# Written tables for the order of five engines in a fused recurrent attention and two-layer kernel

## The chip, the cores and the metric

The kernel runs on one core of one Trainium2 chip. The metric is the device time of one execution in microseconds (us). A core has five engines that run their own lists of instructions in order and wait for each other by semaphores: PE (TensorE, matmuls), ACT (ScalarE), DVE (VectorE), POOL (GpSimd) and SP (SyncE, which here only issues DMA transfers). POOL issues some transfers too.

## The reference

A gated linear recurrence over 768 tokens, for 4 batches of 8 heads with 48 channels each, and a two-layer network on its output.

```python
for t in range(S):
    state = alpha[:, :, t, :, None] * state + np.einsum('bhd,bhe->bhde', k[:, :, t], v[:, :, t])
    y[:, :, t] = np.einsum('bhd,bhde->bhe', q[:, :, t], state)
x = np.ascontiguousarray(y.transpose(0, 2, 1, 3)).reshape(B * S, H * D)
h = x @ w_in                      # 3072 x 384 by 384 x 2048
r = np.maximum(h, 0.0)
out = (r * r) @ w_out             # 2048 x 384
```

Inputs and output are float32; the kernel multiplies in bfloat16.

## The kernel before, in words

The work is cut into 12 units, g = 0 to 11: unit g is batch g mod 4 and the tokens 256 (g div 4) onward, so that units 4 to 7 go on with the states of units 0 to 3, and 8 to 11 with theirs. A unit takes these steps, and each step of the program has a short name with the unit's number, which the prediction uses:

- Loads: lda, ldk, ldq, ldv bring 384 KB each of alpha, k, q and v (L568). SP issues them, for unit 2 POOL. Two halves of w_in (win0, win1) and of w_out (wout0, wout1), 768 KB each, come by POOL's queue (L539). A load has a gate (`AFTER`, `BEHIND`): from unit 4 on all four loads of g wait until ldq of g-1 has landed; lda3 waits for wout0, win0 for lda1; from unit 5 on lda waits also for ln of the unit before, ldk for ekm, ldq and ldv until tr0 of the unit before has landed. SP waits for a gate at the place where the load stands in its list.
- Decays: pr multiplies pairs of alphas (DVE L675 or POOL L677), ln and lm take logarithms (ACT L678, L717), m1i and m1s sum them by a triangular matmul (PE L684, bank psW), ei, ea, ec and es are exponentials of these sums (ACT L695 to L721; units 0 and 1 have forms of their own, L584 to L667), bk, aq and lb are products and differences (DVE).
- ekm and eqm scale k and q (DVE L751, L746, L620). tr transposes them: units 0 to 2 on PE (L632, L774) with evictions et, from unit 3 on by two DMA transposes from SP, tr0 and tr1 (L762).
- p: scores, 32 small matmuls into psX and psZ (PE L940); mk0 and mk1 mask them on DVE (L951, 1.2 us each).
- vc: v to bfloat16 (ACT L742 or POOL L741, L613). y: output matmuls into psX, which from y2 to y10 also hold the state matmuls kv of unit g+1 and therefore need vc of g+1 (PE L832, L843, L811). sa, sc, sd update the states (sd on POOL L915 or DVE L917).
- xe evicts y (ACT L971), xt transposes it (PE L986 for units 0 to 3, a DMA transpose L992 from unit 4 on), xv copies (DVE L998).
- The dense part: s1 is eight blocks of six matmuls (PE L1042) into two banks psH in turn, each emptied by re (ACT L1050 or DVE L1052) and squared by sq (DVE L1060, ACT L1064); s2 is eight blocks of four matmuls (L1089) into psO, emptied by oe (ACT L1097, DVE L1099); out stores (SP L1109).

What sets the order: `add` records each step with its engine or engines to choose from, a cost, a priority, and what it depends on: writers of what it reads, readers of what it overwrites, and, of a PSUM bank (`ps`), all earlier readers of that bank too, so that two readers never meet there. `schedule` simulates the program with these costs and always takes the ready step of least priority; priorities carry hand offsets (`SHIFT`). `fill` then puts 37 matmuls on zeros (fillers, L1143) into PE's list where its simulation sees a gap before the first s1; they wait for the memset of the zero tile. `place` turns dependencies into semaphore waits, leaving out those that another wait already covers; a step of PE never waits for a step of PE, a step of ACT or DVE can wait for one of its own engine. `emit` writes the lists.

```python
            if k[0] == "ps":
                for r in self.readers.get(k, ()):
                    op.deps.setdefault(r, False)
...
                if d.sem is None and d.eng == o.eng == "pe":
                    continue
```

Of the kernel before, what the change touches and what calls it, by code (L numbers as in the profile page):

```python
# [2 lines left out]

# [28 lines left out]


class Program:

    HOP = 35
    PE_LATENCY = 170
    DMA_FIRST = {"sp": 1300, "act": 1300, "pool": 2000}  # L40
    PACKET = (("win", 172), ("wout", 490), ("ld", 22), ("tr", 18), ("xt", 18), ("out", 125))
    SBUF_ONLY = ("pr", "bk", "aq", "ekm", "eqm", "sq", "sb", "sd")
    BIAS = {"pool": 300}
    DMA_LAST = {"sp": 800, "act": 800, "pool": 1900}
    SWITCH = 95
# [1129 lines left out]
```

## Time and profile before

| what | value |
|---|---|
| runs | 176.59, 176.57, 174.76 us; median 176.57 |
| span of the profiled execution, first to last instruction | 174.5 us (the lowest run is 0.3 above it) |
| PE busy | 169.1 us, 97% |
| DVE, ACT, POOL busy | 121.3, 117.6, 18.8 us |
| s1 matmuls L1042 | 576, mean 275 ns |
| s2 matmuls L1089 | 368, mean 326 ns |
| fillers L1143 | 37, 10.5 us |
| DMA moved | 33.36 MB, mean 191 GB/s |
| HBM read, written | 25.17 MB, 4.72 MB |

The profile page gives busy time by engine, the span in 40 slices with a digit for the busy share in tenths, the chain of work that ended last, and groups of instructions with their number and mean time. A matmul's mean holds its way through the array, so that several overlap; what a block of matmuls costs is read from the start of one block to the start of the next. The trace names instructions by line; since every engine runs its list in order, the n-th instruction in the trace is the n-th of the list, and so each step of the program has its time.

### The profile page before, as it was taken

To read this page: it belongs to the slowest core of one execution; us is meant where nothing else is said; L and a number is where in the kernel's file an instruction comes from. 1 tells how busy PE (TensorE), PEld (TensorE's weight loads), DVE (VectorE), ACT (ScalarE), POOL (GpSimd) and SP (SyncE) were. 2 spreads that over 40 slices of the span, in tenths; PEclk is the share of its full clock that TensorE was granted. 3 is DMA by queue.
4 is the path that set the end of the run, shared out by engine and by line. 5 is a ranking of instruction groups with operands and counts; after the bars stand their busy time and mean duration, and the time that the engine had idled before them with its cause. 6 is when DMAs were issued, how large, how long until landed. Compare 5 with 4: busy or idle time off the path is not lost.

```text
span 174.5 us, 5094 instructions
## 1 busy us (share of the span) xinstructions
PE 169.1 (97%) x2237; PEld 130.5 (75%) x2237; DVE 121.3 (70%) x197; ACT 117.6 (67%) x211; POOL 18.8 (11%) x28
## 2 busy tenths in 40 slices
PE   7989999999999999999999999999999999999994
PEld 2556898856886697777788886778788697688773
DVE  5497799797967869866778966868849726322230
ACT  3848698868869569768768757378668564566440
POOL 3159010022102120000100000000200000000000
DMA  5999999979998999798998897999899690040022
GB/s 139 324 297 190 274 303 216 230 208 280 274 229 125 274 235 188 200 222 151 278 212 211 228 196 180 275 201 251 201 214 208 115 196 4 0 135 4 10 80 90
DMA packets 74743, 33.36 MB, mean 191 GB/s; under 512 B 71649, under 2 KB 71905, under 8 KB 74721
## 3 DMA queue, kind: packets, MB, share of 16 engines
q1 hardware_dynamic: 73184, 28.32, 71.4%
q0 software_dynamic: 1536, 4.72, 12.1%
q8 instruction: 17, 0.28, 0.7%
q14 instruction: 6, 0.04, 0.1%
HBM read 25.17 MB, written 4.72 MB: 171 GB/s over the span
## 4 chain that ended last, share of the span: by engine, by line
PE 56%; DMA 26%; ACT 6%; DVE 4%; SPq 3%; POOL 2%; issue 1%
PE psO L1089 22%; PE psWH L1042 22%; DMA raw<-in_v_dram 9%; DMA wout<-in_moe_w_out_dram 8%; DMA raw<-in_alpha_dram 5%; DMA raw<-in_q_dram 5%; SPq L568 3%; PE psO L1143 2%; POOL raw L568 2%; ACT rr L1050 2%; PE psX L843 2%; PE psX L1012 2%; ACT vbf L742 1%; PE psZ L811 1%; PE psX L832 1%; PE psX L940 1%
## 5 line engine op out<-in xcount | busy, mean ns | idle before, releaser
L1042 PE MATMUL psWH<-xt,win 128*128 128x256 bf16 x576 | 73.9, 275 | 0.5 <-ACT rr L1050 0.2
L1042 PEld LDWEIGHTS psWH<-xt,win 128*128 128x128 bf16 x576 | 65.0, 145 | 6.2 <-DVE rr L1052 1.6
L1089 PE MATMUL psO<-wout,gt 128*128 128x384 bf16 x368 | 68.9, 326 | 0.0
L1050 ACT ACTIVATE rr<-psWH 128x512 bf16<-128x512 f32 x83 | 48.9, 596 | 21.5 <-PE psWH L1042 20.0
L1089 PEld LDWEIGHTS psO<-wout,gt 128*128 128x128 bf16 x368 | 34.8, 98 | 18.3 <-DVE gt L1060 0.2
L1060 DVE TENSOR_TENSOR gt<-rr 128x1024 bf16<-128x1024 bf16 (+1 forms) x47 | 28.4, 608 | 25.1 <-ACT rr L1050 24.5
L951 DVE TENSOR_TENSOR pm<-psX,caus 128x1024 bf16<-128x1024 f32 x12 | 14.6, 1220 | 2.4 <-PE psZ L940 2.1
L951 DVE TENSOR_TENSOR pm<-psZ,caus 128x1024 bf16<-128x1024 f32 x12 | 14.6, 1216 | 1.5 <-PE psZ L940 1.4
L1097 ACT ACTIVATE osb<-psO 128x384 f32<-128x384 f32 x19 | 9.3, 489 | 6.8 <-PE psO L1089 6.3
L971 ACT ACTIVATE xbf<-psX 128x768 bf16<-128x768 f32 x12 | 9.7, 806 | 5.0 <-PE psX L832 4.1
L746 DVE TENSOR_TENSOR qks<-raw,eq 128x384 bf16<-128x384 f32 x18 | 10.3, 605 | 3.0 <-DMA raw<-in_q_dram 3.0
L1143 PE MATMUL psO<-zero 128*128 128x512 bf16 (+1 forms) x37 | 10.5, 417 | 1.3 <-DVE zero L489 1.3
L741 POOL CAST vbf<-raw 128x768 bf16<-128x768 f32 x4 | 3.7, 930 | 71.5 <-DMA raw<-in_v_dram 71.5
L1064 ACT ACTIVATE gt<-rr 128x512 bf16<-128x512 bf16 (+1 forms) x13 | 10.8, 828 | 0.4
L751 DVE TENSOR_TENSOR qks<-raw,ek 128x768 bf16<-128x768 f32 x11 | 10.7, 969 | 0.4 <-ACT ek L663 0.3
L1052 DVE TENSOR_SCALAR rr<-psWH 128x512 bf16<-128x512 f32 x13 | 8.9, 687 | 2.0 <-PE psWH L1042 1.6
L742 ACT ACTIVATE vbf<-raw 128x768 bf16<-128x768 f32 x7 | 5.9, 845 | 3.5 <-DMA raw<-in_v_dram 3.5
L717 ACT ACTIVATE la<-raw 128x384 f32<-128x384 f32 x8 | 4.2, 523 | 5.3 <-DMA raw<-in_alpha_dram 5.2
L1143 PEld LDWEIGHTS psO<-zero 128*128 128x128 bf16 x37 | 3.5, 108 | 4.6 <-issue 1.9
L906 DVE TENSOR_TENSOR smd<-psZ,sbd 128x384 bf16<-128x384 f32 x8 | 4.4, 554 | 3.4 <-PE psX L832 3.4
L675 DVE TENSOR_TENSOR prd<-raw 128x384 f32<-128x384 f32 x7 | 4.0, 569 | 2.9 <-DMA raw<-in_alpha_dram 2.9
L678 ACT ACTIVATE lab<-prd 128x384 bf16<-128x384 f32 x10 | 5.2, 520 | 1.1 <-POOL prd L677 0.6
(115 smaller groups left out, 165.9 us busy)
## 6 DMA issues: line engine op xcount, KB each, us to landing
raw<-in_alpha_dram SPq DMA_DIRECT2D x11, 384.0 KB, 4.2
raw<-in_k_dram SPq DMA_DIRECT2D x11, 384.0 KB, 5.1
raw<-in_q_dram SPq DMA_DIRECT2D x11, 384.0 KB, 4.2
raw<-in_v_dram SPq DMA_DIRECT2D x11, 384.0 KB, 4.8
out_dram<-osb SPq DMA_DIRECT2D x11, 384.0 KB, 4.3
win<-in_moe_w_in_dram POOLq DMA_DIRECT2D x2, 768.0 KB, 9.9
wout<-in_moe_w_out_dram POOLq DMA_DIRECT2D x2, 768.0 KB, 15.2
raw<-in_alpha_dram POOLq DMA_DIRECT2D x1, 384.0 KB, 9.7
```

Source lines behind the costliest of these rows:

```text
L746: add("dve", lambda e, j=j, dst=dst: e.tensor_tensor(dst, RAW[r][:, 2, :, j, :].rearrange("p (n x) d -> p n x d", x=2), EQ[la][:, j].rearr ...
L751: add("dve", lambda e, a=a, E=E: e.tensor_tensor(QKS[qs][:, a, :, :, 0:D], RAW[r][:, 1 + a].rearrange("p h j d -> p j h d"), E[la][:].rear ...
L951: add("dve", lambda e, hf=hf, psT=psT: e.tensor_tensor(PM[pm][:, hf].rearrange("p r n j t -> p (r n) (j t)"), psT[:, :, :].rearrange("p r ...
L971: add("act", lambda e: e.activation(XBF[x2][:], psX[:, :, 0:HD], AF.Copy), act_ns(2 * HD), p0 + 6100, reads=[("ps", "X", 0), ("ps", "X", 1 ...
L1042: ins = pe.matmul(psH[hb][:, i * T:(i + 1) * T], WIN[:, kk, hidden(fj)], mov, start=(kk == 0), stop=(kk == KT - 1))
L1050: add("act", lambda e, hb=hb, rr=rr: e.activation(rr, psH[hb], AF.Relu), act_ns(512), pu + 600, reads=[("ps", "H", hb)], writes=[("rr", rb ...
L1052: alts={"dve": (lambda e, hb=hb, rr=rr: e.tensor_scalar(rr, psH[hb], 0.0, None, ALU.max), dve_ns(512))})
L1060: add("dve", lambda e, dst=dst, sq=sq: e.tensor_tensor(dst, sq, sq, ALU.mult), 148 + k * 267, pu + 1200, reads=[("rr", rb, h) for h in ran ...
L1064: "act": (lambda e, dst=dst, sq=sq: e.activation(dst, sq, AF.Square), act_ns(k * 512))})
L1089: ins = pe.matmul(psS, GT[gt][:, fj, j, :], WOUT[:, fj, :], start=(fj * parts % FT == 0), stop=((fj + 1) * parts % FT == 0))
L1097: add("act", lambda e, j=j, psS=psS: e.activation(OSB[ob][:, j], psS, AF.Copy), act_ns(DM), ps_ + 700, reads=[keyS], writes=[("osb", ob, j ...
L1143: pr.fill(lambda n: lambda pe: pe.matmul(psO[:, 0:n], ZERO[:, 0:128], ZERO[:, 0:n], skip_group_check=True), ((512, 216, 420), (256, 109, 2 ...
```

## The change

The scheduler, its constants and its offsets go, and `fill` with them. The five orders stand in the kernel as text, `TABLES`, and `arrange` takes each step's engine and place from there; `+512` and `+256` in PE's table are fillers. `sequence` gives `place` an order of all steps that keeps every dependency. `place` leaves out one more kind of wait: of a step on an earlier step of its own engine when the only reason was that both read the same bank. Readers on different engines still wait for each other. The steps themselves, their tiles and their arithmetic are the same; 20 steps go from ACT to DVE and vc6 to POOL; 24 come to ACT from DVE, vc0 and vc5 from POOL; sd1, sd2, pr5 and pr6 go from POOL to DVE; POOL's list shrinks from 24 to 19, PE's fillers from 37 to 23.

```diff
                 for r in self.readers.get(k, ()):
-                    op.deps.setdefault(r, False)
+                    if r not in op.deps:
+                        op.deps[r] = False
+                        op.shared.add(r)
...
             for r in self.readers.get(k, ()):
                 if r is not op:
                     op.deps.setdefault(r, False)
+                    op.shared.discard(r)
...
-                if d.sem is None and d.eng == o.eng == "pe":
+                if d.sem is None and d.eng == o.eng and (o.eng == "pe" or not raw and d in o.shared):
                     continue
...
+    def arrange(self, tables, make, after):
...
+            for x in text.split():
+                if x[0] == "+":
+                    o = Op({e: (make(int(x[1:])), 0)}, 0, "fill")
...
+                    o.deps = {after: True}
...
+                o.eng = e
+                o.fn, o.cost = o.alts[e]
+                o.pos = len(self.order[e])
+                self.order[e].append(o)
```

The lists of before, for the places that the prediction names:

```
pool ... vc0 win0 win1 sd0 lda2 ldk2 ldq2 ldv2 wout0 wout1 sd1 pr3 sd2 vc4 pr5 vc5 pr6 vc7 vc10
sp   lda0 ldk0 ldq0 ldv0 lda1 ldk1 ldq1 ldv1 lda3 ldk3 ldq3 ldv3 lda4 ldk4 ldq4 ldv4 out0_1 tr0_3 tr1_3 lda5
     ldk5 tr0_4 tr1_4 ldq5 ldv5 out1_1 lda6 ldk6 tr0_5 tr1_5 out2_1 xt4 ldq6 ldv6 lda7 ldk7 tr0_6 tr1_6 xt5
     ldq7 ldv7 out3_1 lda8 ldk8 tr0_7 tr1_7 out4_1 xt6 ldq8 ldv8 ...
pe   9 fillers, m10_0 m11_0, 4 fillers, tr00_0, 2 fillers, tr10_0, 3 fillers, tr01_0 p0_0 kv0 tr11_0 ...
     y5 s2_3_1_0 s1_4_5 s2_3_1_1 s2_3_1_2 s1_4_7 s2_3_1_3 s1_4_4 m1i7 ...
act  table, xcaus, ln0_0 ln1_0 ei0_0 ea0_0 ei1_0 ... xe2 lm4 ln4 ... re4_0 re4_1 vc6 re4_2 re4_3 xe5 lm7 ln7 ...
dve  zero first, sixteen memsets, ekm0_0 eqm0_0 et00_0 ekm1_0 eqm1_0 mk0_0 sa0 sc0 mk1_0 ekm1 eqm1 xv0 et0_1 ...
```

The same places after it:

```diff
+TABLES = {
+    "act": """
+        table xcaus ln1_0 ln0_0 ei1_0 ea1_0 ei0_0 ec1_0 ea0_0 ec0_0 vc0 ln1 et11_0 ei1 ea1 ec1 vc1 xe0 et0_1
...
+        sq1_5 re1_6 sq1_6 ln3 oe0_0 ei3 ea3 ec3 vc3 oe0_1 es3 lm4 xe2 ln4 sa3 xv2 ei4 ea4 oe1_0 ec4 re2_1 re2_0
+        es4 re2_3 lm5 re2_2 ln5 re2_5 re2_4 sq2_5 re2_7 re2_6 ei5 sq2_7 oe1_1 ea5 ec5 xe3 es5 xv3 vc5 re3_0
+        re3_1 lm6 sq3_1 re3_2 re3_3 ln6 re3_4 xe4 ei6 re3_6 ea6 ec6 oe2_1 re3_5 es6 sq3_5 re3_7 sq3_7 re4_0 lm7
+        re4_1 ln7 xe5 oe3_0 ei7 re4_3 ea7 re4_2 ec7 es7 re4_4 re4_5 sq4_5 re4_6 re4_7 sq4_6 re5_0 re5_1 re5_2
...
+    "dve": """
+        zcaus1 zlstr zcaus zlinc zqk0 zones zlb1 zlb0 zqk1 zla0 zident zla1 zown zqk2 zown0 zero zown1 ekm1_0
+        eqm1_0 ekm0_0 eqm0_0 et00_0 et10_0 et01_0 sa0 mk0_0 sc0 mk1_0 ekm1 eqm1 xv0 et1_1 mk1_1 mk0_1 sa1 sq0_1
...
+    "pe": """
+        +512 +512 +512 +512 +512 m11_0 m10_0 +512 +512 +512 +256 +256 tr00_0 tr10_0 tr01_0 kv0 p0_0 tr11_0 m11
+        p1_0 +512 +512 +512 +512 +512 +512 y0 tr0_1 +512 xt0 tr1_1 +512 +512 +512 +256 p0_1 +256 +256 s1_0_0
...
+        s2_2_0_2 s2_2_0_3 s1_3_0 s1_3_1 p0_4 s1_3_2 s1_3_3 s2_2_1_0 s2_2_1_1 s1_3_4 y4 m1i6 s1_3_6 s2_2_1_2
+        s2_2_1_3 s1_3_5 p0_5 s2_3_0_0 s2_3_0_1 s1_3_7 s2_3_0_2 s1_4_0 s1_4_1 y5 s2_3_0_3 m1i7 s1_4_3 s1_4_2
+        s2_3_1_0 s2_3_1_1 s2_3_1_2 s1_4_4 s1_4_5 p0_6 s1_4_6 s1_4_7 s2_3_1_3 s1_5_0 s1_5_1 s2_4_0_0 s1_5_2
...
+    "pool": """
+        scaus1 slinc scaus sident slstr win0 win1 sd0 lda2 ldk2 wout0 ldq2 ldv2 wout1 pr3 vc4 vc6 vc7 vc10
+    """,
+    "sp": """
+        lda0 ldk0 ldq0 ldv0 lda1 ldq1 ldk1 ldv1 lda3 ldq3 ldk3 ldv3 ldq4 lda4 ldv4 ldk4 out0_1 tr1_3 lda5 tr0_3
+        ldk5 tr0_4 tr1_4 ldq5 ldv5 out1_1 lda6 ldk6 tr0_5 tr1_5 ldv6 ldq6 xt4 out2_1 lda7 ldk7 tr1_6 tr0_6 xt5
+        ldv7 ldq7 out3_1 lda8 ldk8 tr1_7 tr0_7 xt6 ldq8 ldv8 out4_1 lda9 ldk9 tr1_8 tr0_8 xt7 ldq9 ldv9 out5_1
+        ldk10 lda10 tr0_9 tr1_9 xt8 ldq10 ldv10 out6_1 lda11 ldk11 tr1_10 tr0_10 xt9 ldq11 ldv11 out7_1 tr1_11
+        tr0_11 xt10 out8_1 xt11 out9_1 out10_1 out11_0 out11_10 out11_11
```

More of the change, by code (lines that the diff above doesn't have):

```diff
@@ L1 @@
-import heapq
-import itertools
 import concourse.bass as bass
@@ L15 @@
 class Op:
-    __slots__ = ("alts", "eng", "fn", "cost", "prio", "deps", "idx", "lag", "sem", "start", "end", "pos", "name",
-                 "users", "ndeps", "mode", "ready", "land")
+    __slots__ = ("alts", "eng", "fn", "cost", "prio", "deps", "idx", "lag", "sem", "pos", "name", "mode", "shared")
     def __init__(self, alts, prio, name):
@@ L26, in __init__ @@
         self.sem = None
-        self.users = []
         self.pos = None
         self.mode = ("F", "F")
-        self.ready = 0.0
-        self.start = self.end = self.land = None
+        self.shared = set()
 class Program:
[L38 to L45, printed above, removed]
-    HALVED = {"qks": 3, "kqt": 3, "raw": 3, "ek": 3, "eq": 3, "acm": 2, "laf": 2}
-    AFFINITY = 2500
-    SHIFT = {
[55 rows of a table removed]
-    }
+    HALVED = {"qks": 3, "kqt": 3, "raw": 3, "ek": 3, "eq": 3, "acm": 2, "laf": 2}
     def __init__(self, nc):
@@ L113, in __init__ @@
         self.dma_count = {}
-        self.filler = None
+        self.fills = {}
     def add(self, eng, fn, cost, prio, reads=(), writes=(), name="", dma=None, lag=0, after=(), mode=("F", "F"),
@@ L123, in add @@
             choices.update(alts)
-        op = Op(choices, prio + self.SHIFT.get(name, 0), name)
+        op = Op(choices, prio, name)
         op.idx = len(self.ops)
@@ L271, in fill @@
-    def fill(self, make, sizes, until, after, cold):
-        new = []
-        t = after.land + self.HOP
-        cold += t
-        for o in self.order["pe"]:
-            while t < until:
-                slow = 2 if t < cold else 1
-                fits = [(n, c) for n, c, gap in sizes if o.start - t > gap + (slow - 1) * c]
-                if not fits:
-                    break
-                n, c = fits[0]
-                f = Op({"pe": (make(n), c)}, 0, "fill")
-                f.idx = len(self.ops)
-                f.eng, f.fn, f.cost = "pe", make(n), c
-                f.start, f.end = t, t + c * slow
-                f.deps = {after: True}
-                self.ops.append(f)
-                new.append(f)
-                t = f.end
-            new.append(o)
-            t = max(t, o.end)
-        for i, o in enumerate(new):
-            o.pos = i
-        self.order["pe"] = new
+    def arrange(self, tables, make, after):
+        named = {o.name: o for o in self.ops}
+        assert len(named) == len(self.ops)
+        self.order = {}
+        for e, text in tables.items():
+            self.order[e] = []
+            for x in text.split():
+                if x[0] == "+":
+                    o = Op({e: (make(int(x[1:])), 0)}, 0, "fill")
+                    o.idx = len(self.ops)
+                    o.deps = {after: True}
+                    self.ops.append(o)
+                else:
+                    o = named.pop(x)
+                o.eng = e
+                o.fn, o.cost = o.alts[e]
+                o.pos = len(self.order[e])
+                self.order[e].append(o)
+        assert not named, sorted(named)
@@ new lines, in sequence @@
+    def sequence(self):
+        done, seq = set(), []
+        at = {e: 0 for e in self.order}
+        while len(seq) < len(self.ops):
+            before = len(seq)
+            for e, ops in self.order.items():
+                while at[e] < len(ops) and all(d in done for d in ops[at[e]].deps):
+                    o = ops[at[e]]
+                    done.add(o)
+                    seq.append(o)
+                    at[e] += 1
+            assert len(seq) > before, {e: ops[at[e]].name for e, ops in self.order.items() if at[e] < len(ops)}
+        return seq
@@ L301, in place @@
         waits = {}
-        seq = sorted(self.ops, key=lambda o: (o.start, o.idx))
+        seq = self.sequence()
+        rank = {o: i for i, o in enumerate(seq)}
         needed = set()
@@ L322, in place @@
             mine = []
-            for d in sorted(want.values(), key=lambda d: -d.start):
+            for d in sorted(want.values(), key=lambda d: -rank[d]):
                 s, p = stream(d), place_of(d)
@@ L351, in emit @@
         stores = {}
-        for o in sorted((o for o in self.ops if o.name.startswith("out")), key=lambda o: o.start):
-            stores.pop(o.sem[0], None)
-            stores[o.sem[0]] = o
+        for o in self.order["sp"]:
+            if o.name.startswith("out"):
+                stores[o.sem[0]] = o
         final = [(self.dma_sems[k], self.value[o]) for k, o in stores.items()]
@@ L504, in bass_gla_recurrent__then__act_relu_squared_kernel @@
                           (flat[0], "caus", 1.0), (flat[1], "caus1", 1.0), (ONES2[:], "ones", 1.0)):
-        add("dve", fill(buf, val), 100, -2.5e6, writes=[(key,)])
-    add("pool", select(LINC[:], ALU.is_ge, 0.0, 0, [[1, 128]], -1), 300, -1e6, reads=[("linc",)], writes=[("linc",)])
-    add("pool", select(LSTR[:], ALU.is_gt, 0.0, 0, [[1, 128]], -1), 300, -1e6, reads=[("lstr",)], writes=[("lstr",)])
-    add("dve", fill(OWN[:], 0.0), 100, -2e6, writes=[("own",)])
-    for part in (OWN[0:64, 0:H:2], OWN[64:128, 1:H:2]):
-        add("dve", fill(part, 1.0), 100, -2e6, reads=[("own",)], writes=[("own",)])
-    zero = add("dve", fill(ZERO[:], 0.0), 300, -3e6, writes=[("zero",)])
+        add("dve", fill(buf, val), 100, -2.5e6, writes=[(key,)], name="z" + key)
+    add("pool", select(LINC[:], ALU.is_ge, 0.0, 0, [[1, 128]], -1), 300, -1e6, reads=[("linc",)], writes=[("linc",)], name="slinc")
+    add("pool", select(LSTR[:], ALU.is_gt, 0.0, 0, [[1, 128]], -1), 300, -1e6, reads=[("lstr",)], writes=[("lstr",)], name="slstr")
+    add("dve", fill(OWN[:], 0.0), 100, -2e6, writes=[("own",)], name="zown")
+    for x, part in enumerate((OWN[0:64, 0:H:2], OWN[64:128, 1:H:2])):
+        add("dve", fill(part, 1.0), 100, -2e6, reads=[("own",)], writes=[("own",)], name=f"zown{x}")
+    zero = add("dve", fill(ZERO[:], 0.0), 300, -3e6, writes=[("zero",)], name="zero")
     add("pool", select(IDENT[:], ALU.not_equal, 1.0, 0, [[-1, 128]], 1), 300, -1e6 + 5, reads=[("ident",)],
-        writes=[("ident",)])
+        writes=[("ident",)], name="sident")
     for c, key in enumerate(("caus", "caus1")):
         add("pool", select(flat[c], ALU.is_ge, 0.0, 128 * c, [[-1, 2], [1, 2], [2, 64]], -2), 400, -1e6 + 7,
-            reads=[(key,)], writes=[(key,)])
+            reads=[(key,)], writes=[(key,)], name="s" + key)
     add("act", lambda e: e.activation(flat[1][0:64], flat[0][0:64], AF.Copy), 400, -1e6 + 8,
-        reads=[("caus",), ("caus1",)], writes=[("caus1",)])
+        reads=[("caus",), ("caus1",)], writes=[("caus1",)], name="xcaus")
     def bcast(t, row, dims):
@@ L1141, in bass_gla_recurrent__then__act_relu_squared_kernel @@
             moe(g)
-    pr.schedule()
-    pr.fill(lambda n: lambda pe: pe.matmul(psO[:, 0:n], ZERO[:, 0:128], ZERO[:, 0:n], skip_group_check=True),
-            ((512, 216, 420), (256, 109, 250)), min(o.start for o in pr.order["pe"] if o.name.startswith("s1_")), zero, 4600)
+    pr.arrange(TABLES, lambda n: lambda pe: pe.matmul(psO[:, 0:n], ZERO[:, 0:128], ZERO[:, 0:n], skip_group_check=True),
+               zero)
     pr.place()
```

146 lines of the change are left out of this document (39 added, 107 removed), and 55 rows, old and new, of the table SHIFT.

## The prediction

> **What bounds the kernel now.** I read the page first: busy shares, the row of DMA slices, the chain that ended last.
>
> ```profile
> span 174.5 us, 5094 instructions
> ...
> PE 169.1 (97%) x2237; PEld 130.5 (75%) x2237; DVE 121.3 (70%) x197; ACT 117.6 (67%) x211; POOL 18.8 (11%) x28
> ...
> DMA  5999999979998999798998897999899690040022
> ...
> PE 56%; DMA 26%; ACT 6%; DVE 4%; SPq 3%; POOL 2%; issue 1%
> ```
>
> PE is busy 97% of the span, and DMA is nearly full until slice 32 of 40 (140 us). The chain is mostly PE with DMA between. A busy PE need not be at its pace, so I took each block's start to the next block's start from the timeline: an s1 block takes 0.655 us, an s2 block 0.650, a y block 1.05, a p block 0.573, m1i 0.27. From the first s1 at 18.46 to the last matmul at 172.1, only these exceed their pace by more than the 0.1 of a change of tiling: 0.40 at 26.6, about 0.7 in sum around m1s2, kv2, m1i3 and m1s3 (28 to 40), 0.15 at 65.5, 0.37 at 73.2, 0.25 at 98.6, 0.41 at 114.3, 0.27 at 116.3, 0.23 at 150.9. That is 2.8 us: no order of the same blocks can win more behind the first s1, and any block that comes up before its input lands loses at once, because PE runs its list in order.
>
> Next the chain in order of time, for what a late block waits on.
>
> ```profile
> 16.73 13.68 DMA wout<-in_moe_w_out_dram
> ...
> 34.10 5.31 DMA raw<-in_v_dram
> 39.44 0.85 ACT vbf L742
> ...
> 80.13 4.17 DMA raw<-in_q_dram
> 84.31 4.31 DMA raw<-in_alpha_dram
> 88.64 0.57 DVE prd L675
> 89.23 0.53 ACT lab L678
> ```
>
> Unit 3's loads wait for wout0 (landed 30.41); later lda(g+1) is issued only when ldq(g) has landed. Last the timelines of SP, ACT and PE around unit 7, where the new order differs most.
>
> ```profile
> 59.82 5.00 SPq L762 DMA_TRANSPOSE kqt<-qks  x2
> 64.86 1.20 SPq L1109 DMA_DIRECT2D out_dram<-osb  x1
> 66.10 1.42 SPq L992 DMA_TRANSPOSE xt<-xbf  x1
> 67.57 0.59 SPq L568 DMA_DIRECT2D raw<-in_q_dram  x1
> 68.20 0.65 SPq L568 DMA_DIRECT2D raw<-in_v_dram  x1
> 72.12 0.37 SPq L568 DMA_DIRECT2D raw<-in_alpha_dram  x1
> ```
>
> ```profile
> 76.27 0.53 ACT L717 ACTIVATE la<-raw 128x384 f32<-128x384 f32 x1
> 76.87 0.52 ACT L678 ACTIVATE lab<-prd 128x384 bf16<-128x384 f32 x1
> ```
>
> ```profile
> 79.97 0.33 PE L684 MATMUL psWH<-lab,linc 128*128 128x384 bf16 x1
> ```
>
> lda7 is issued at 72.12 and lands 4.13 later; ln7 ends at 77.39; m1i7 runs at 79.97. So m1i7 has 2.6 us of slack today.
>
> **The change part by part.** Names below are the program's; times of the trace of before belong to them by counting each engine's instructions off against its list.
>
> Waits: the program of before holds 21 waits of ACT on its own earlier read of the same bank (ei to ea, ea to ec). After one, ACT starts 0.03 after the end (6.53 to 6.56); without one it starts 0.10 before the end (ea0_0 ends 7.05, ei1_0 starts 6.95). So 21 x 0.13 = 2.7 us of ACT, which is busy 67%: hidden by its idle time, 0 taken, at most 0.13 a unit on the way to the loads' transposes.
>
> Evictions, squares and copies (re, sq, oe, et, xv) change sides between ACT and DVE, five more on ACT: each has about the same price on both (re 0.60 and 0.69, sq of 1024 1.06 and 0.71), and both engines idle 30% or more: 0.
>
> Scheduler and filler code: it ran while the program was built, 0. Fillers go from 37 to 23; they stand only where PE waits anyway, 0, except in the head.
>
> Head. The memset of zero moves from first to sixteenth on DVE: the memsets ahead of it take 2.5 us, so fillers start at about 3.45 instead of 1.25. Their rate in the trace is 427 ns a 512-column matmul until 5.07, then 216: half speed for 3.8 us. Five of them end at 3.45 + 2.14 = 5.6, so the first m1 starts 0.5 late and runs at half speed; ei1_0 follows at 6.5, 0.5 later than ei0_0 does now. This is regained: vc0 goes from POOL to ACT, and beside POOL's cast ekm1_0 took 1.21 against 0.56 for its like (0.65 back); et1_1 goes from ACT (1.03) to DVE (0.68). Step by step from those rows: mk1_0 ends 13.8 (now 13.43), y0 starts 13.85 (13.48), xt0 15.6 (15.50), xv0 ends 16.7 (16.59), et1_1 17.3 (17.83), p0_1 17.35 (17.88), two fillers, first s1 18.15 (18.46). win0 lands 17.91, which excludes more than -0.55. I take -0.3. If PE stays at half speed longer, the tr, kv0 and p0 blocks on that path take some 0.6 more: ends -0.5 and +0.3.
> The Trainium skill, "TensorE: Matmul & The Clock Gate", section "What's actually happening", asks for one whole busy window of about 3.4 us, free-running. By it the full clock could come as late as two windows behind the first filler, 10.3, where the row's 3.8 us give 7.25; the sum would then be 0.6 higher. No run here shows which.
>
> Stage 26 to 45. wout0 moves ahead of ldq2 and ldv2 on POOL's queue. Today it lands 3.56 after ldv2; ahead of them it lands at 24.73 (ldk2) + 3.56 = 28.3, and lda3 is issued 2.1 earlier. The bytes up to ldv3 are the same, so ldv3 (39.41 now) gains between 0.3 and 1.2; y2, which waited for vc3 behind it, starts at about 39.85 instead of 40.42. q2 and v2 land about 4 later, near 30 and 31; eqm2 (30.67) and the s1 blocks behind vc2 on ACT still find them: 0, up to +0.8. But on ACT lm4 now stands ahead of xe2, and lm4 waits for lda4 (40.6 to 41.5): xt2 up to 0.55 late, +0.25 taken. Standing at 45 us: -0.3 - 0.3 + 0.25 = -0.35, ends -0.8 and +0.8.
>
> Moves off POOL. sd1, sd2, pr5, pr6 go to DVE (0.56 each, 2.2 us; DVE is busy 70%), vc5 to ACT, vc6 to POOL. DVE's work is covered by its waits for ACT (24.5 us at L1060). vc6 can hold eqm0_6 up: beside a cast eqm0_7 took 0.86 against 0.55, ekm1_0 lost 0.65. Ends 0 and 0.65, on tr1_6, which has more slack than that; 0 taken.
> The Trainium skill, "SBUF — State Buffer", calls the shared port pair an exclusive lock held for the whole instruction. By that ekm1_0, which began 0.02 after the 0.82 cast, would lose 0.80; the row says 0.65, so the row is used.
>
> Unit 7, the costly step. Ahead of m1i7 PE's list loses five s1 and four s2 blocks: 5 x 0.655 + 4 x 0.650 = 5.88. PE comes up at 79.97 - 5.88 = 74.09; less the idle of before on the way (0.37, 0.15) and the standing of -0.35, at 73.2. What m1i7 needs: on SP, ldq3 stands second in its unit and lands 1.2 earlier, which lets ldq4 and lda4 go; lda5 stands ahead of tr0_3 and goes at about 43.9 (46.53 now); ldk5 still waits for ekm4, goes at 46.3, lands 4.4 later at 50.7, and tr0_4, which lands 1.1 behind it (54.51 and 53.38 now), at 51.8. That is 2.7 earlier, and ldq5, which waits for that landing, lda6, tr0_5 and ldq6 inherit it; out2_1 and xt4 move behind ldq6, but ldq6 waits for tr0_5 to land (66.78 now) and gains nothing from their place. So lda7 at about 69.5 (72.12). It lands 4.1 later, 73.6; then ACT does lm7 (0.53), re4_1 (0.60), ln7 (0.52): 75.25. m1i7 stalls 75.25 - 73.2 = 2.05, and the dense blocks behind it wait too, s1_4_3 above all, whose bank re4_1 empties behind lm7. Net at m1i7: 75.25 - 74.09 = +1.15. Ends: no lead at all, ln7 77.9, +3.8; a lead of 4.7, no stall, -0.9. I take the lead that the SP rows give.
>
> Units 8 to 11. tr1 goes ahead of tr0 for units 6 to 8, and ldq waits for tr0's landing: the second landing is 0.8 to 2.3 behind the first, about what moving "out" behind the loads (1.3) gives back: 0. p0_8, p0_10, y11 come up 3.9, 4.1, 4.6 earlier in PE's list. tr1_10 lands 132.19 for p0_10 at 133.10; with the lead of about 2 and PE 1.15 later, 0.9 + 2 + 1.15 = 4.05 against 4.1: on the edge, +0.3 taken. The idle of before in this part (0.25 + 0.41 + 0.27 + 0.23 = 1.16) came from loads that now lead: 0.9 won. Net -0.6, ends -1.16 and +1. The tail (last s1 to the end) keeps its blocks: 0.
>
> Sum: +1.15 - 0.6 = +0.55 us against a span of 174.5: 175.05. The lowest run, 174.76, is 0.3 above that span, the median 176.57 is 2.1 above; against the median it is 177.1.
>
> **Rivals.**
> Slower: the loads don't lead. If lda7 is issued at 72.1 as now, ln7 ends 77.9, net +3.8 - 0.6 = +3.2: 179.8. For it: DMA's slices are full there, so an earlier issue need not land earlier, and tr0_5 took 7 us to land. Against: SP waited 15.6 us for q loads in seven places, so the chain of landings has room. It decides where ln7 ends behind 76.4, that is lda7 issued behind 70.7.
> Faster: the loads lead by over 4 us and m1i7 finds ln7 done: -0.9 there and all 1.16 of the later idle gone: -2.05, 174.5. For it: the place of m1i7 fits such a lead. Against: no row gives more than 2.7.
> Not what it says: the dropped waits bring nothing, as costed; that leaves the forecast as it is. Longer half speed in the head gives 177.7, also within no change.
>
> **How the numbers follow.** Within 1% (174.8 to 178.3, about what a measurement tells from no change): 0.44, the forecast, 177.1. Slower by over 1%: 0.34. Faster by over 1%: 0.22, bounded by the 2.8 us of idle and the 0.5 of the head. The likeliest case's own range is 174.8 to 178.3; the range reaches down to 173.9, below the faster rival by half a microsecond, and up to 180.2, past the slower one.
>
> **What would show it.** Right: first s1 near 18.15; lda3 near 28.3; y2 before 40.42; lda7 near 69.5 and PE idle of about 2 us just ahead of m1i7 (L684, x10), released by ACT's lab. Wrong: a first s1 behind 18.8 (clock), PE idle at s1 blocks behind lm5, or at p0 blocks waiting for transposes; an lda7 outside 67.5 to 71; and idle in sum under 1 us or over 5 us behind the first s1.

## The result and the profile after

| | before | after |
|---|---|---|
| median | 175.94 us (4 runs, 174.76 to 176.59) | 181.1 us (4 runs, 180.51 to 181.77) |
| span of the profiled execution (its own time) | 174.5 us | 179.4 us (181.16) |
| PE idle behind the first s1, beyond the blocks' paces | 1.75 us | 6.71 us |
| dense blocks (s1, s2) behind y11 in PE's list | 29 | 36 |
| y11 starts, then to the start of the last s2 block | 150.71, 20.5 us | 151.07, 25.0 us |

The ratio is 1.031, 95% interval 1.024 to 1.0381: slower, where no change was forecast. PE's idle is worked out as in the prediction, from the start of a block to the start of the next less the block's pace; what is over 0.12 counts, and the sums take 0.1 for the change of tiling off each. The page of after:

```profile
span 179.4 us, 5067 instructions
...
PE 166.6 (93%) x2223; PEld 129.1 (72%) x2223; DVE 117.4 (65%) x197; ACT 118.7 (66%) x216; POOL 13.3 (7%) x23
...
DMA  5999999999997999976895999979988292202022
...
DMA 49%; PE 30%; DVE 7%; ACT 6%; SPq 3%; issue 1%; POOL 1%
```

PE's share fell from 97% to 93%, and the chain that ended last has turned over: DMA 26% before, 49% now. In order of time, start and length, the chain around units 5 to 7:

```profile
44.40 3.93 DMA raw<-in_alpha_dram
48.33 6.23 DMA kqt<-qks
...
54.57 3.42 DMA raw<-in_q_dram
...
65.85 5.69 DMA raw<-in_q_dram
...
71.55 3.78 DMA raw<-in_alpha_dram
...
75.35 0.52 ACT la L605
...
76.26 0.52 ACT lab L566
...
76.83 0.34 PE psWH L572
```

lda5 is early, as intended (44.40; 46.53 before). But the transpose tr0_4 lands at 54.56 (54.51 before), so ldq5 goes when it always went, and lda7 at 71.55 against 72.12. SP's issues of after from lda5 to the two transposes of unit 4 (lda5, tr0_3, ldk5, then tr0_4 and tr1_4) leave no gap:

```profile
44.40 0.53 SPq L456 DMA_DIRECT2D raw<-in_alpha_dram  x1
44.97 2.11 SPq L650 DMA_TRANSPOSE kqt<-qks  x1
47.13 1.15 SPq L456 DMA_DIRECT2D raw<-in_k_dram  x1
48.33 3.80 SPq L650 DMA_TRANSPOSE kqt<-qks  x2
```

PE's list now calls the attention's blocks up to nine dense blocks earlier. Yet lda comes only 0.75 and 0.57 us earlier in units 6 and 7, and 1.2 to 2.2 us later from unit 8 on: lda8 at 85.75 (84.31), lda10 at 111.54 (109.39). Two views show where PE paid. First ACT; the bracket gives the idle time ahead of an instruction and what ended it:

```profile
48.62 0.53 ACT L605 ACTIVATE la<-raw 128x384 f32<-128x384 f32 x1 [0.58 <-DMA raw<-in_alpha_dram]
...
59.26 0.84 ACT L630 ACTIVATE vbf<-raw 128x768 bf16<-128x768 f32 x1 [1.53 <-DMA raw<-in_v_dram]
60.01 1.07 ACT L938 ACTIVATE rr<-psWH 128x512 bf16<-128x512 f32 x2
62.61 0.52 ACT L605 ACTIVATE la<-raw 128x384 f32<-128x384 f32 x1 [1.54 <-DMA raw<-in_alpha_dram]
63.04 1.04 ACT L952 ACTIVATE gt<-rr 128x1024 bf16<-128x1024 bf16 x1
63.99 1.06 ACT L938 ACTIVATE rr<-psWH 128x512 bf16<-128x512 f32 x2
...
128.99 0.52 ACT L605 ACTIVATE la<-raw 128x384 f32<-128x384 f32 x1 [2.48 <-DMA raw<-in_alpha_dram]
129.42 0.47 ACT L985 ACTIVATE osb<-psO 128x384 f32<-128x384 f32 x1
```

These are lm5, vc5, lm6 and lm11, each standing in ACT's list ahead of an eviction (L938, L985) whose data is ready. ACT waits for the load with it, and PE for the eviction:

```profile
60.64 1.53 PE L930 MATMUL psWH<-xt,win 128*128 128x256 bf16 x12 [0.58 <-ACT rr L938]
...
64.62 0.88 PE L930 MATMUL psWH<-xt,win 128*128 128x256 bf16 x6 [1.15 <-ACT rr L938]
...
129.95 0.82 PE L977 MATMUL psO<-wout,gt 128*128 128x384 bf16 x4 [1.51 <-ACT osb L985]
```

By place PE's idle is 0.64 up to 40 us, 1.27 at 40 to 60, 2.20 at 60 to 80 (s1_3_4 at 64.62, y4 and m1i7; s1_3_2 at 60.64 is in the part before), 0.45 at 100 to 120 (m1i10), 2.02 at 120 to 140. Second, SP's waits (sum, times, longest), after and then before:

```profile
SPq L997 <- ACT osb L985: 23.9, 7, 9.4
...
SPq L456 <- DMA kqt<-qks: 6.5, 5, 2.4
```

```profile
SPq L1109 <- ACT osb L1097: 11.0, 2, 10.3
...
SPq L568 <- DMA kqt<-qks: 0.7, 1, 0.7
```

These sums hold much that costs nothing: 20.2 of the 23.9 us, and all 11.0 of before, are waits of the stores out7_1 to out10_1, issued when no load is left. Ahead of the last load out2_1, out4_1 and out5_1 waited 3.8 us in after, out3_1 4.3 more (under another line), where before had no such wait. In both lists the store out3_1 stands ahead of lda8; its oe3_1 now ends at 85.32 instead of 80.01, so that lda8 goes at 85.75 though ldq7 landed at 84.59. And ldq8 waits 2.0 us for tr0_7, which became the second of two transposes.

DMA itself, in windows (the first column is the window; the last two are DMA's share, which can come out over 1, and GB/s), before and after:

```profile
80.00:100.00 20.00, 19.91 (x300) 15.82 (x299) 16.74 (x25) 15.54 (x30) 0.82 (x1) 1.00 0.97 220
20.00:140.00 120.00, 118.93 (x1656) 93.53 (x1658) 96.71 (x148) 88.57 (x161) 9.03 (x9) 1.00 0.99 221
```

```profile
80.00:100.00 20.00, 20.00 (x268) 16.68 (x267) 15.63 (x26) 14.09 (x26) 0.83 (x1) 1.00 0.85 195
20.00:140.00 120.00, 114.39 (x1587) 90.04 (x1586) 91.17 (x145) 86.01 (x161) 4.30 (x5) 1.00 0.98 217
```

Over these 120 us DMA's share is 0.99 and 0.98, with the same bytes to bring in the whole run (33.36 MB). Loads that all come 2.7 us earlier would find little room in it. At 80 to 100 us, though, DMA isn't full in after: its share is 0.85, and 195 GB/s against 220 are 0.5 MB less in 20 us. There SP held loads back (lda8 behind out3_1, ldq8 behind tr0_7), so part of the lateness of units 8 to 11 comes from SP's list and not from a full DMA.

### The profile page after: what moved, and what is told of

Same layout as the page of the kernel before. It is cut to its first block, busy times and chain, and to the rows that moved or that the text cites. A ratio compares the mean times of both kernels' runs of the same rounds, so it can differ in the third digit from the quotient of the medians.

```text
span 179.4 us, 5067 instructions
## 1 busy us (share of the span) xinstructions
PE 166.6 (93%) x2223; PEld 129.1 (72%) x2223; DVE 117.4 (65%) x197; ACT 118.7 (66%) x216; POOL 13.3 (7%) x23
## 2 busy tenths in 40 slices
DMA packets 74742, 33.36 MB, mean 186 GB/s; under 512 B 71648, under 2 KB 71904, under 8 KB 74720
## 3 DMA queue, kind: packets, MB, share of 16 engines
q1 hardware_dynamic: 73184, 28.32, 70.7%
## 4 chain that ended last, share of the span: by engine, by line
DMA 49%; PE 30%; DVE 7%; ACT 6%; SPq 3%; issue 1%; POOL 1%
DMA kqt<-qks 14%; DMA raw<-in_q_dram 13%; PE psWH L930 12%; DMA raw<-in_alpha_dram 12%; PE psO L977 12%; DMA wout<-in_moe_w_out_dram 7%; DMA raw<-in_v_dram 3%; SPq L650 2%; PE psX L900 1%; PE psO L1030 1%; DVE pm L839 1%; SPq L456 1%; ACT rr L938 1%; POOL raw L456 1%; ACT gt L952 1%
## 5 line engine op out<-in xcount | busy, mean ns | idle before, releaser
L938 ACT ACTIVATE rr<-psWH 128x512 bf16<-128x512 f32 x85 | 50.1, 595 | 19.2 <-PE psWH L930 17.5
L977 PEld LDWEIGHTS psO<-wout,gt 128*128 128x128 bf16 x368 | 34.8, 98 | 20.2 <-ACT osb L985 1.6
L948 DVE TENSOR_TENSOR gt<-rr 128x1024 bf16<-128x1024 bf16 (+1 forms) x44 | 25.5, 586 | 24.2 <-ACT rr L938 24.1
L985 ACT ACTIVATE osb<-psO 128x384 f32<-128x384 f32 x21 | 10.3, 489 | 9.5 <-PE psO L977 9.3
L952 ACT ACTIVATE gt<-rr 128x1024 bf16<-128x1024 bf16 (+1 forms) x16 | 13.9, 871 | 0.7 <-DVE rr L940 0.3
L563 DVE TENSOR_TENSOR prd<-raw 128x384 f32<-128x384 f32 x9 | 5.0, 556 | 10.9 <-DMA raw<-in_alpha_dram 10.9
L634 DVE TENSOR_TENSOR qks<-raw,eq 128x384 bf16<-128x384 f32 x18 | 9.5, 553 | 3.2 <-DMA raw<-in_q_dram 1.8
L1030 PE MATMUL psO<-zero 128*128 128x512 bf16 (+1 forms) x23 | 6.5, 410 | 3.5 <-DVE zero L377 3.5
L940 DVE TENSOR_SCALAR rr<-psWH 128x512 bf16<-128x512 f32 x11 | 7.5, 686 | 0.3 <-PE psWH L930 0.2
L609 ACT ACTIVATE eq<-la 128x384 f32<-128x384 f32 x8 | 4.2, 519 | 3.0 <-DVE la L607 3.0
L1030 PEld LDWEIGHTS psO<-zero 128*128 128x128 bf16 x23 | 2.0, 105 | 5.6 <-DVE zero L377 3.5
```

The lines of the kernel that those rows point to most:

```text
L634: add("dve", lambda e, j=j, dst=dst: e.tensor_tensor(dst, RAW[r][:, 2, :, j, :].rearrange("p (n x) d -> p n x d", x=2), EQ[la][:, j].rearr ...
L938: add("act", lambda e, hb=hb, rr=rr: e.activation(rr, psH[hb], AF.Relu), act_ns(512), pu + 600, reads=[("ps", "H", hb)], writes=[("rr", rb ...
L940: alts={"dve": (lambda e, hb=hb, rr=rr: e.tensor_scalar(rr, psH[hb], 0.0, None, ALU.max), dve_ns(512))})
L948: add("dve", lambda e, dst=dst, sq=sq: e.tensor_tensor(dst, sq, sq, ALU.mult), 148 + k * 267, pu + 1200, reads=[("rr", rb, h) for h in ran ...
L952: "act": (lambda e, dst=dst, sq=sq: e.activation(dst, sq, AF.Square), act_ns(k * 512))})
L977: ins = pe.matmul(psS, GT[gt][:, fj, j, :], WOUT[:, fj, :], start=(fj * parts % FT == 0), stop=((fj + 1) * parts % FT == 0))
```

## The experiments

Theory **L**: SP's new order makes the ring of loads and transposes late. Theory **A**: ACT's head-of-line waits lose the time. Theory **R** (P in the expectations that were put on record first): PE's list calls the attention early while dense blocks that could run are kept for the end. Theory **D** came last: DMA is full, so y11 cannot come before about 150 us, and a list with seven more dense blocks (7 x 0.65 = 4.6 us) behind y11 ends that much later.

**The dropped waits and the new program.** `lists_before`: the lists of before as `TABLES`, POOL's, ACT's and DVE's among them; the 21 waits stay dropped.

> The five lists of before written as tables in the changed program, so that only the dropped waits of ACT on itself and the way the program is built differ from before. All three theories expect the time of before within 0.5%, 175.0 to 176.8 us, and PE idle behind the first s1 near 2.8 us: 21 waits of 0.13 us on an engine that is busy 67%. If the time is over 1% away from before in either direction, the dropped waits or the table machinery matter and the theories start from the wrong place.

Measured 176.03 us, 1.0034 (0.9985 to 1.0083), y11 at 150.0. The whole loss is in the tables.

**SP's order, and ACT's.** `sp_before` is after with SP's list of before, `sp_only` before's lists with the new list of SP, `act_moves` after with eight steps of ACT put behind the evictions that PE waits for:

```diff
-... lm5 re2_2 ... vc5 re3_0 re3_1 lm6 sq3_1 re3_2 ... lm7 re4_1 ... lm11 oe7_0 ...
+... re2_2 lm5 ... re3_0 vc5 re3_1 sq3_1 re3_2 lm6 ... re4_1 lm7 ... oe7_0 lm11 ...
```

> The changed kernel with SP's list of before alone put back. Theory L (SP's new order makes the loads land later: ldv ahead of ldq, tr1 ahead of tr0, lda behind other work): lda8 to lda11 are issued 1.3 us earlier or more than in the changed kernel, and the time falls by 2 to 4 us, to 177 to 179. Theory A (ACT's list, load-dependent steps ahead of evictions) and theory P (PE's list calls attention blocks too early): the loads land within 0.5 of where they did or the gain is lost again, 180 to 182.

> The lists of before with SP's new list alone. Theory L: the loads of units 7 to 11 are issued 1 to 2 us later than in before, and the kernel loses 2 to 4 us, to 178 to 180. Theories A and P: the old ACT and PE lists have the slack for it, within 1 us of before, 175 to 177.

> The changed kernel with eight load-dependent steps of ACT moved behind the evictions that they held up: lm4 behind xe2, lm5 behind re2_2, vc5 behind re3_0, lm6 behind re3_2, lm7 behind re4_1, lm10 behind xe8, lm11 behind oe7_0, vc11 behind sq8_7; nothing else. Theory A: the idle of PE at s1 and s2 blocks behind them (0.4, 0.5, 0.65, 1.3, 0.2, 1.6, 0.4, in sum 5 us) goes, time 176 to 177.5. Theory L: the loop of loads and transposes sets the pace, the idle comes back at m1i, p and y blocks, gain 1.5 us at most, 179.5 to 181. Theory P: as L.

`sp_before`: 205.22 us, 1.1545 (1.141 to 1.168). Its PE waits, among others:

```profile
PE psWH L928 <- DMA xt<-xbf: 11.9, 5, 4.2
```

SP's list is no separate part: the old one has stores ahead of loads (SP waits 49.3 us for osb, about 30 of them ahead of loads) that the new PE list fills later. `sp_only`: 179.89, 1.0233 (1.0158 to 1.0307); tr0_3, now behind tr1_3 and lda5, lands at 52.67 (48.04) and p0_3 costs 2.27 of idle, y11 comes at 155.3. The same move cost nothing in `sp_lda5` below, where tr1_3 went at 42.37 and not at 44.00, so the move alone isn't what costs here. `act_moves`: 1.0296 (1.021 to 1.0381). It won 1.7 us up to y6 (86.05 against 87.77), since no eviction waited behind a load, and had lost them again at y11 (150.68 against 151.07): p0_8 waited 1.10, s1_8_2 1.66. So A is right about the places and wrong about the sum: PE came earlier to blocks whose loads were no earlier.

**Mending the ring.** `sp_fix`: tr0 ahead of tr1 again for units 3, 6, 7, 8, 10, ldq ahead of ldv, lda10 ahead of ldk10, out2 to out7 behind the next lda and ldk. `sp_fix_act`: that with `act_moves`. `nogate_after`: no gate of ldq and ldv on tr0.

```diff
-... tr1_7 tr0_7 xt6 ldq8 ldv8 out4_1 lda9 ldk9 ...
+... tr0_7 tr1_7 xt6 ldq8 ldv8 lda9 ldk9 out4_1 ...
```

```diff
-    BEHIND = {"a": "ln", "k": "ekm", "q": "tr0_", "v": "tr0_"}
+    BEHIND = {"a": "ln", "k": "ekm"}
```

> The changed kernel with four kinds of move in SP's list: tr0 ahead of tr1 for units 3, 6, 7, 8 and 10, ldq ahead of ldv for units 6 and 7, lda10 ahead of ldk10, and the stores out2_1 to out7_1 behind the next lda and ldk. Theory L (the loop lda, tr, ldq, lda sets the pace and SP's list lengthens it): the round from lda6 to lda11, 65.6 us in the changed kernel and 63.6 in before, falls below 63.6, and the time to 177 to 179. Theory P (PE's list calls attention blocks too early for any such loop): the round shortens by less than 1 us or the time stays, 180 to 182.

> sp_fix with the eight moves of act_moves as well. Theory L: act_moves gave 1.7 us by y6 and lost it again where the transposes of unit 8 came late; with the loop shortened it is kept, so 175 to 177, about the time of before. If theory A still has a part, sp_fix_act is faster than sp_fix by 1.5 us or more. Theory P: 179 to 182.

> The changed kernel without the gate of ldq(g) and ldv(g) on tr0 of the unit before having landed; the buffers' own dependencies stay. Theory L (the changed order of tr1 and tr0 keeps the loads back): ldq8 and ldq9 are issued about 2 us earlier, lda10 and lda11 come 2 earlier, y11 at about 149 and the time 178.5 to 179.5. Theory R: the loads do come earlier, but part of it lands behind blocks that PE calls too early anyway; 179.5 to 181. Without effect (the transposes themselves wait for the loads in DMA): 181.

1.0381 (1.0257 to 1.0506), 1.0306 (1.0189 to 1.0422), 1.0212 (1.015 to 1.0274). None wins what L hoped for; `nogate_after` may win up to a point, but its interval overlaps that of after. `sp_fix` made the stretch from lda6 to lda11 1.2 us shorter (64.4 against 65.6) but PE stood idle for 4.3 us at 40 to 60 us (1.27 in after), 2.48 of them at s1_2_4 alone: lda5 had gone back behind tr0_3 while the other lists counted on it early.

**Early data.** `half_after` and `half_before`: the loads of units 4 to 11 bring 64 of 128 partitions (half of that input is left out), with the new and with the old lists.

```diff
+            if g >= 4:
+                dst, src = dst[0:64], src[0:64]
```

> The changed kernel, but the loads of units 4 to 11 bring only the first 64 of 128 partitions (half the packets and bytes; the rest of a tile keeps an older unit's data, so half of the input of these units is left out). All waits and lists stay. Theory L: with loads that land early PE's list has no holes left, idle of PE behind the first s1 falls from 7 to under 3.5 us, time 175 to 177, no slower than half_before by more than 1 us. Theory P: idle stays over 5 us, and it is still 4 us behind half_before.

> The lists of before (as in lists_before) with the same half loads from unit 4 on, the same part left out. Both theories: loads no longer end a wait of PE behind unit 3, 1 to 2 us gained at most, 174 to 175.5; it is the yardstick for half_after.

175.25, 0.9968 (0.9927 to 1.0009), and 174.77, 0.9942 (0.9903 to 0.9982). The window of `half_after`:

```profile
20.00:140.00 120.00, 118.80 (x1674) 94.72 (x1675) 93.10 (x147) 90.61 (x167) 4.72 (x5) 1.00 0.83 169
```

DMA's share falls to 0.83, the idle of PE behind the first s1 from 6.71 to 1.6 us, and the loss of the new lists from 3.1% to about 0.3%. y11 now starts at 145.17 with the new lists, at 149.18 with the old: with data in time the new lists do bring the attention 4.0 us ahead, about the seven blocks, and the dense work kept for the end costs nothing. These two runs show the cause as far as this: the lists ask for loads that come too late for them. Why the loads can't come earlier they don't settle, since half the bytes both empty DMA and shorten each load (lda lands 3.8 us after its issue in the median, 4.6 in after): L expected the same result. For a full DMA speak its share of 0.98, and `sp_lda5` below; against its being the whole reason speaks the share of 0.85 at 80 to 100 us.

**Filling PE's idle.** `pe_moves`: nine dense blocks moved ahead to where PE stood idle, m1i10 a block back; `pe_act_moves`: with `act_moves`.

```diff
-... p0_4 s1_3_2 s1_3_3 s2_2_1_0 s2_2_1_1 s1_3_4 y4 m1i6 s1_3_6 s2_2_1_2 s2_2_1_3 s1_3_5 ...
+... p0_4 s2_2_1_0 s1_3_2 s1_3_3 s2_2_1_1 s2_2_1_2 s2_2_1_3 s1_3_4 y4 m1i6 s1_3_6 s1_3_5 ...
```

> The changed kernel with ten dense blocks of PE's list moved a few places ahead, each to just before a block at which PE stood idle there (s2_1_0_2 ahead of xt2, s2_1_1_2 ahead of s1_2_4, s2_2_1_0 ahead of s1_3_2, s2_2_1_2 and s2_2_1_3 ahead of s1_3_4, s1_4_2 ahead of m1i7, s1_8_4 and s1_8_3 ahead of s2_7_1_0, s2_8_0_3 ahead of s1_9_2), and m1i10 one block back. Nothing else moves. Theory R (PE's list calls blocks before their inputs land while dense blocks that could run stand behind them): the idle at these places falls from about 6 us to about 3, and the time to 177 to 179. Rival L (the ring of loads, transposes and decays sets the time, whatever PE does between): the idle moves to the next block of the attention, and the time stays within 180.5 to 182.

> The PE moves of the last kernel and, beside them, eight steps of ACT's list (lm5, vc5, lm6, lm11, vc11 and their like) moved behind the evictions that PE waits for. Theory R: either move alone lets the other list's early call hold PE; together the idle behind the first s1 falls under 3.5 us and the time to 175.5 to 178. Rival L: the ring sets the time, 180 to 182.

1.0438 (1.0341 to 1.0534) and 1.0282 (1.0217 to 1.0347): R fell. y11 started at 151.8 and 151.2 all the same; the idle had moved to other blocks. The moves left 36 blocks behind y11.

**Dense work ahead, en bloc.** `dense_early`: in PE's, ACT's and DVE's lists the dense steps stand up to 4.6 us ahead of the attention's, so that 30 blocks are left behind y11.

```diff
-... s2_6_0_3 s1_7_4 y8 s1_7_6 s2_6_1_0 s2_6_1_1 m1i10 s2_6_1_2 s2_6_1_3 p0_9 s1_7_5 s2_7_0_0 ...
+... s2_6_0_3 s1_7_4 s1_7_6 s2_6_1_0 s2_6_1_1 s2_6_1_2 s2_6_1_3 y8 s1_7_5 s2_7_0_0 s2_7_0_1 s1_7_7 m1i10 ...
```

> The changed kernel with the dense steps alone (s1 and s2 on PE, re, sq and oe on ACT and DVE) moved ahead of the attention's steps: by nothing at 45 us, by 4.6 us from 77 us on, by the starts in the trace of after. 30 dense blocks are left behind y11 in PE's list instead of 36 (before: 29). SP's list, the sides and the order within each class stay. Theory D (DMA is full, so y11 can't come before 150 to 151 us; the new lists ask for the attention some 4.6 us ahead of its data): y11 stays at 150.5 to 151.5, the idle behind the first s1 falls to 2.5 to 4, the time to 176.5 to 178. Rival S (SP's new order itself loses the time): y11 moves to 153 or later, 180 to 182.

207.52, 1.167 (1.157 to 1.1771), y11 at 178.9: D's number fell too.

```profile
PE psWH L928 <- DMA xt<-xbf: 13.1, 7, 3.8
```

I had let s1 follow its y by 3 us, but xt lands 8 behind it (y6 at 87.77, xt6 at 96.00 in after). So s1 waited for xt, the attention behind it in PE's list came late, and the loads that hang on the attention with it; DMA's share at 20 to 140 us fell to 0.87. The edit was too coarse to test the last part of D, but it shows the other side of the ring: a dense block too early costs as a block of the attention does.

**Order or sides.** `assign_only`: order of before, each of 51 steps on its new engine at its old start. `order_only`: the reverse.

```diff
-pool ... wout0 wout1 sd1 pr3 sd2 vc4 pr5 vc5 pr6 vc7 vc10
-act  ... re3_0 oe2_1 lm6 re3_1 ln6 ...
+pool ... wout0 wout1 pr3 vc4 vc6 vc7 vc10
+act  ... re3_0 vc5 oe2_1 re3_2 lm6 re3_1 sq3_1 ln6 ...
```

> The lists of before, with the 51 steps that change their engine put on the new engine at the place of their old start. Theory D: the sides cost nothing, 175.5 to 177. Rival E (the new sides lose: vc5 on ACT, pr5, pr6, sd1 and sd2 on DVE): 178.5 to 181.

> The lists of after, with the same 51 steps back on the engines of before at the place of their start in after. Theory D: the order alone costs what the change costs, 179.5 to 182. Rival E: 176 to 178.

1.0179 (1.0098 to 1.026) and 1.0427 (1.0363 to 1.0491). Against D the sides cost by themselves, 1.0% to 2.6%, and the order without its sides costs no less than with them, probably more (1.0427 against 1.031, the intervals overlap a little). That both were made for each other fits this and isn't shown by it. In `assign_only` vc5 stands ahead of oe2_1, re3_2 and lm6 on ACT, and PE loses 1.65 us around m1i6 (66 us); lda6 goes 1.5 late, y11 comes at 154.2. Which of the 51 steps does it was not taken apart.

**The one step of SP, and the place of the loss.** `head_y2`: the new lists up to 41 us, then those of before; `head_y2_again`: the same kernel, run more often; `sp_lda5`: `head_y2` with the step from which the prediction took its lead; `head_y4`: the new lists up to 66.5 us.

```diff
-... ldk4 out0_1 tr0_3 tr1_3 lda5 ldk5 tr0_4 tr1_4 ldq5 ...
+... ldk4 out0_1 tr1_3 lda5 tr0_3 ldk5 tr0_4 tr1_4 ldq5 ...
```

> The changed lists up to y2 (about 41 us), the lists of before behind it, in the changed program. If the loss lies wholly behind 41 us, as the map of steps has it, this kernel takes 175 to 176.5 (before 175.9) and may win the 0.4 of the head and of y2. If the early part already costs something that shows only later, 177 or more.

> The kernel of head_y2 (new lists up to 41 us, those of before behind them), with one move of SP's list more: lda5 ahead of tr0_3, with tr1_3 ahead of it, as in the changed kernel. By the prediction's step the landing of tr0_4 and with it lda7 come 2 or more us earlier (lda7 at 69 or before, head_y2 70.98). By theory D the DMA engines are full and tr0_4 is held by eqm0_4 as well: lda5 lands 1.5 earlier, tr0_3 2 to 3 later (p0_3 waits), tr0_4 within 0.6 of head_y2 and lda7 not earlier than 70.5; time 176 to 178.

> The same kernel as head_y2 (ratio 0.9968, interval 0.9926 to 1.001). If the new head and the earlier wout0 are a gain of their own, as lda7 at 70.98 and y11 at 149.29 say, the ratio is 0.993 to 0.998 and its interval stays below 1.000; else 1.000.

> The changed lists up to 66.5 us (just behind y4 and m1i6), the lists of before behind them. In the changed kernel PE's idle behind the first s1 up to there is 3.7 us, against about 1.0 in before. If an idle PE is never regained (it is busy 97% in before), the time is 175.9 + 2.7 - 0.4 for the head = 178 to 179. If the lists of before give it back, since they have 2.8 us of idle themselves: 175.5 to 177.

SP's issues in `head_y2`, then in `sp_lda5`:

```profile
45.90 1.10 SPq L454 DMA_DIRECT2D raw<-in_alpha_dram  x1
47.05 0.63 SPq L454 DMA_DIRECT2D raw<-in_k_dram  x1
47.72 4.89 SPq L648 DMA_TRANSPOSE kqt<-qks  x2
53.56 0.53 SPq L454 DMA_DIRECT2D raw<-in_q_dram  x1
...
70.98 0.37 SPq L454 DMA_DIRECT2D raw<-in_alpha_dram  x1
```

```profile
44.03 0.82 SPq L454 DMA_DIRECT2D raw<-in_alpha_dram  x1
44.89 1.97 SPq L648 DMA_TRANSPOSE kqt<-qks  x1
46.91 1.06 SPq L454 DMA_DIRECT2D raw<-in_k_dram  x1
48.01 5.09 SPq L648 DMA_TRANSPOSE kqt<-qks  x2
54.19 0.37 SPq L454 DMA_DIRECT2D raw<-in_q_dram  x1
...
71.58 0.37 SPq L454 DMA_DIRECT2D raw<-in_alpha_dram  x1
```

lda5 goes 1.87 earlier, ldk5 0.14, and tr0_4 0.29 later; lda7 is 0.60 later. How much of this is the move? In the profile of `head_y2_again`, the same kernel as `head_y2`, lda7 goes at 71.87 and y11 starts at 151.09 (149.29 in `head_y2`), so two executions differ by 0.9 and 1.8 us there, and 0.60 later is within that. What the prediction had put on this move, a lead of 2.7, isn't there against either profile: one load ahead of others brings the later ones no lead. Times: `head_y2` 0.9968 (0.9926 to 1.001), again 0.9987 (0.9952 to 1.0023), `sp_lda5` 0.9979 (0.9944 to 1.0015): all as before, so the new head costs nothing and gains nothing that can be measured; no version beat both kernels. `head_y4`: 1.0124 (1.0089 to 1.016), 2.2 us. PE's idle in it is 4.81 us in sum (before 1.75), 3.93 of them at 40 to 80 us. Behind 80 us it is 0.29, where before has 0.76, so the old lists give back half a microsecond and no more. The other 3 us or so of the change (181.1 less 175.9 less 2.2) arise behind 66 us.

## Why the prediction was wrong

- Head: right. First s1 at 18.09 (forecast 18.15), fillers from 3.47 (3.45), p0_1 at 17.29 (17.35).
- Stage 26 to 45: right. lda3 at 27.95 (28.3), ldv3 landed 38.71 (38.2 to 39.1), y2 at 39.81 (39.85), xt2 0.38 late behind lm4 (0.25).
- Waits, sides, machinery at 0: right for the waits (`lists_before`). Wrong for the sides: 1.8% alone in `assign_only`. vc5's move to ACT got no price of its own; what counted was its place, ahead of re3_0, with v5 landing at 59.23.
- Unit 7: **the failed step is "That is 2.7 earlier, and ldq5, which waits for that landing, lda6, tr0_5 and ldq6 inherit it."** It had ldk5 issued at 46.3, landing 4.4 later, and tr0_4's landing 1.1 behind that, at 51.8. But tr0_3, put behind lda5, holds SP for 2.11 us, so ldk5 went at 47.13; it landed 5.0 later at 52.11 (53.38 before), and tr0_4 2.45 behind it, at 54.56. tr0_4 was issued when it always was (48.33, 48.44 before), right behind ldk5's issue; eqm0_4, which it needs, was hardly earlier (ended at 48.01, 48.13 before; DVE's new order puts sq2_1 ahead of it). Its landing took 6.2 us (6.1 before). The Trainium skill, "DMA: Bandwidth & Descriptors", section "Queues, rings and completion order", has each DMA engine consume one queue's descriptors in ring order; the trace agrees as far as lda5, tr0_3, ldk5 and tr0_4 land in the order of their issue (48.60, 49.42, 52.11, 54.56). lda7 came at 71.55, past the 70.7 that the prediction gave as the point from which its slower rival decides.
- m1i7's stall was 0.97, not 2.05, because PE itself came up at 75.86 and not 73.2: s1_2_4, s1_3_2 and s1_3_4 had waited 0.48, 0.65 and 1.31 on the way. These waits, and 1.58 at s2_7_1_0 later, were not in the sum; they come from ACT's list, which I read for what it adds and not for what stands behind a load in it. Three of the prediction's own signs of being wrong came: idle behind lm5, lda7 past 71, over 5 us of idle.
- Units 8 to 11: -0.6 forecast, on the same lead. The loads came 1.2 to 2.2 late instead, and m1i10 and s2_7_1_0 waited 0.55 and 1.58. That moving out behind the loads gives back what tr0 loses did not hold at unit 8: lda8 lost 1.16 to out3_1, and ldq8 went 2.0 later (95.32, 93.31), at tr0_7's landing.
- In the terms of the sum: m1i7 ran 2.7 behind its 74.09 (+1.15 forecast). y11 started 4.9 behind 146.1, its start before less seven blocks, so units 8 to 11 added 2.2 (-0.6 forecast). The two misses, 1.6 and 2.8 us, are the whole miss of 4.4 in the span (179.4 against 175.05), and the larger one lies behind unit 7.
- Rivals: the slower one ("the loads don't lead", 179.8) was right in its mechanism and short by 1.3 us. That it came so near is partly luck: its +3.8 up to m1i7 was 1.1 too much, its -0.6 behind m1i7 was 2.8 too little. Its argument, that DMA's slices are full, should have outweighed SP's 15.6 us of waiting for q: that wait of the issuer was no spare room in the queue.

Open: what the sides cost step by step, how the lateness of the loads divides between a full DMA and SP's own order, and whether 29 blocks behind y11 with the rest of the new order would give the time back (`dense_early` did not test it cleanly).

## What to carry to other kernels

Where PE is busy 97% and DMA 99% over the same stretch, an earlier issue of one load brought the later ones no lead here, and an order that asked for data seven blocks (4.6 us) earlier lost 4.9 us by the last of them. Before believing a lead, take the landing that gates it and ask what issues it and how full the queue is, then look in every in-order list for ready work behind a step that waits for a load. Lists made together are changed together: with SP's list alone swapped the time was 2% (`sp_only`) and 15% (`sp_before`) above that of before.
